# Banded attention, then four experts: loads in another order, x part T4 at the head of its queue, and low halves held back a round

## The chip, the core and the metric

One core of a Trainium2 chip runs the whole program in one launch. The metric is the device time of that launch in microseconds (us); lower is better. The core has five instruction streams that run side by side and wait for each other by semaphores: PE (TensorE, matmuls; its weight loads are listed as PEld), DVE (VectorE), ACT (ScalarE), POOL (GpSimd) and SP, which here only issues transfers. Every stream executes its own instructions strictly in the order in which the program wrote them.

## The reference

```python
# attention: 4 batches, 8 heads, 576 positions, 64 wide
scores = q @ k.T / 8                     # per batch and head
mask_plain = (rel >= 0) & (rel < 32)                       # heads 0..3
mask_dil   = (rel >= 0) & (rel < 128) & (rel % 4 == 0)     # heads 4..7
attn = softmax(where(mask, scores, -1e9))
x = (attn @ v) laid out as [2304, 512]
# mixture of experts: 4 experts, each 512 -> 1024 -> 512
p = domain_probs / domain_probs.sum(-1)
out = sum over e of p[:, e] * (relu(x @ w1[e]) @ w2[e])
```

All of it is float32 with float32 results.

## The kernel before

**Attention** is cut into 24 steps of two groups each (192 queries of a pair of heads). A step needs a load of q (`q_s`) and k (`k_s`, L270), both on SP, and two loads of v (`v_s`, L277). It runs through stages: `s_qk` (scores `sc`, PE, L292), `s_max` (DVE, L306), `s_sub` (POOL, L320), `s_exp` (ACT), `s_sum` (DVE), `s_norm` (POOL, L342), `s_tr` (PE, `pt`), `s_av` (PE, `po`, L373), and ACT copies the result into x. In each *round* (the loop over `n` in the main part) one step is in each stage. q and k have `QKB` = 3 buffers, v has `VB` = 4.

**The experts** are 16 units (four of each expert's four slices of 256 hidden columns), and the 2304 tokens are three blocks m of 768. A *visit* is a unit on a block. Float32 products are made of three products of split numbers: a *high half* (ACT, `HI = copy`, names `xh`, `g1h`, `g2h`, `w2h`, L129) and a *low half*, the rest (POOL or DVE subtract, names `xl`, `g1l`, `g2l`, `w2l`, L126); `split` writes both. The first matmul layer uses a Winograd scheme of seven products (`m1x`, `m1y`, L411) per visit: A12, A11, S2, S1, S3, S4, A22, each with a part of x (B21, B11, T2, T1, T3, B22, T4). The parts T are sums of quarters of x (`x_sums`, DVE, L223), the weights S are sums of quarters of w1 (`w1_sums`, POOL, L160 to L166, in place in the loaded tile `r`). The second layer (`mm2`, result `m`, L514) is scaled into `acc` by DVE (L522). Units 0 and 1 go over block 0 first, with eight plain products each, then units 2 to 15 over block 0 while attention goes on, then all units over blocks 1 and 2.

Weights come in tiles `r`: w1 (L107) with two buffers, w2 (L115) with one. `fetch_w1(u + 2)` is written behind `w1_late(u)`, and `fetch_w2(u + 1)` behind `w2_late(u)`, so SP waits there until POOL has read the buffer (`g2l` or `w2l`); SP's loads written behind them wait as well.

**What sets the order.** Attention's loads stand in the list `loads`; at the head of each round they are issued from its front as long as the buffers allow (`ready`). The splitting of weights and of x goes through `queue`, a list of generators: `step()` takes one step of the first one, and after each piece of expert work (a *tick*) one or two steps are taken; `need(...)` takes steps until a named item is done. From `START` = round 7 to `OPEN` = round 15 (the gate) attention is denser and the experts run two pieces a round; from round 15 on, 11 pieces (`PACE`). `held`, `holding` and `flush()` let `split` write the high half now and the low half later. `dummies` are matmuls without use that keep PE busy early on.

Of the kernel before, what the change touches and what calls it, by code (L numbers as in the profile page):

```python
# [24 lines left out]
VB = 4  # L25
# [24 lines left out]
def kernel(  # L50
# [483 lines left out]
    def experts(begin):  # L534

        for half in range(2):
            for n in ("X12", "B22") if half else ("B11", "B21"):
                for i in range(2):
                    need(x_part, i, n)
            for u in range(2):  # L540
                need(w1_split, u)
                yield from plain((u, 0), half)
                if half:
                    prepare(w1_split, u + 2)
                    prepare(w1_sums, u + 2)
                    if u == 0:
                        prepare(w1_late, 2)
                        fetch_w1(3)
                    else:
                        for j in range(2):  # L550
                            prepare(x_part, j, "T4")
                need(w2_late, u)
                yield from mm2((u, 0), u == 0, False, half, range(2))
                if half:
                    prepare(w2_late, u + 2)
            if half == 0:
                yield from pause("open")
        need(w1_split, visits[0][0])
        yield from mm1_a(visits[0])
        for i, (u, m) in enumerate(visits):  # L560
            blocks = [b for v, b in visits if v == u]
            mine = [v for v in visits if v[1] == m]
            ends = m and (u, m) == mine[0], (u, m) == mine[-1]
            if m == blocks[0]:
                need(w1_late, u)
            yield from mm1_b((u, m))
            if m == blocks[-1] and u < LAST:
                prepare(w1_late, u + 1)
            if (u, m) == (NU - 1, 0):
                for n in ("T3", "T4"):  # L570
                    for j in (4, 5):
                        prepare(x_part, j, n)
            if m == blocks[-1] and u + 2 <= LAST:
                prepare(w1_split, u + 2)
                prepare(w1_sums, u + 2)
            if i + 1 < len(visits):

                need(w1_split, visits[i + 1][0])
                need_x(visits[i + 1][1], ("B11", "B21"))
                opening = mm1_a(visits[i + 1])  # L580
                yield next(opening)
            if m == blocks[0]:
                need(w2_late, u)
            yield from mm2((u, m), *ends, 1)
            if i + 1 < len(visits):
                begin()
                yield from opening
                if visits[i + 1] == (NU - 1, 0):

                    assert "m1" in gate  # L590
                    need(x_sums, 5)
                    for n in ("T2", "T1"):
                        for j in (4, 5):
                            prepare(x_part, j, n)
            yield from mm2((u, m), *ends, 0)
            if m == blocks[-1] and u + 2 <= LAST:
                prepare(w2_late, u + 2)
# [6 lines left out]
    def step(of=None):  # L604
        of = queue if of is None else of
        while of:
            if next(of[0][1], 0) != 0:
                return
            of.pop(0)

    def prepare(what, *args, soon=False, of=None):
        of = queue if of is None else of
        of.insert(0 if soon else len(of), ((what, args), what(*args)))
# [13 lines left out]
    with tc.manual_schedule():  # L627
# [139 lines left out]
        shares = []  # L767
        ready = {"w2": lambda u: u < 1 or (u - 1, 1) in w2_op}
        ready["qk"] = lambda m: m < qk_done + QKB
        ready["v"] = lambda m: m < av_done + VB  # L770

        def load(what, m):
            if what == "qk":
# [8 lines left out]
                (fetch_w1 if what == "w1" else fetch_w2)(m)  # L782

        loads = [
# [5 lines left out]
        ]  # L790
        for m in range(needed[1] + 1, len(steps)):
            loads += [("qk", m), ("v", m)]

        dummies(18)
        ffn = experts(begin)
        for n in range(at(len(steps) - 1) + 5):
            while loads and ready.get(loads[0][0], lambda m: True)(loads[0][1]):
                load(*loads.pop(0))
            if START < n < OPEN:
                flush()  # L800
                holding.add(n)
                step()
                holding.clear()
            for k, order in enumerate(stages):
                for stage, after in order:
                    m = step_at.get(n - after, -1)
                    if m >= 0 and k == (m > needed[1]):
                        stage(m, steps[m])
                        av_done += stage == order[(1, 2)[k]][0]
            if n in step_at:  # L810
                qk_done += 1
            for i, names in when.get(n, ()):
                for name in names:
                    of = first_x if i < 2 else later
                    if name is None or name == "T2":
                        prepare(x_sums, i, of=of)
                    if name is not None:
                        prepare(x_part, i, name.upper(), of=of)
            place = 0 if n <= START or n >= OPEN else len(queue)
            queue[place:place] = first_x  # L820
            first_x.clear()
            if n == 5:
                prepare(w1_split, 0)
            if n == START:
                prepare(w2_late, 0)
                prepare(w1_split, 1)
                weigh(shares[0])
            if n == START + 2:
                prepare(w2_late, 1)
            if n == OPEN:  # L830
                gate.add("open")
            if n < START:
                dummies(FILL)
                step()
                if n > 4:
                    step()
                    step()
                continue
            if "open" not in gate:
                for _ in range(2):  # L840
                    if next(ffn) == "idle":
                        dummies(3)
                    step()
                continue
            for _ in range(PACE if n in step_at else 4):
                next(ffn)
                step()
                if len(queue) > 8:
                    step()
                elif later and len(queue) < 5:  # L850
                    step(later)
# [61 lines left out]
```

## Time and profile before

| | |
|---|---|
| median of 3 runs | 887.48 us (886.26 to 889.19) |
| the profiled execution: its own time | 888.0 us |
| its span, first to last instruction | 886.2 us |
| mean granted TensorE clock | 0.973 |
| PE busy | 833.6 us (94% of the span) |
| DVE / ACT / POOL busy | 479.9 / 315.2 / 390.2 us |
| the chain that ended last | PE 82%, DMA 5% (all of `k_s<-kT`), POOL 4%, DVE 3% |

[...] The 1.8 us between the span and the execution's own time lie outside the instructions.

### The profile page before, as it was taken

The page shows a single profiled execution, that of the slowest core. Times are in us where ns is not written, and L with a number is a line of the kernel's source. Part 1 is how long each engine was busy: PE and PEld are TensorE (multiplying, and loading weights), DVE is VectorE, ACT ScalarE, POOL GpSimd, SP SyncE. Part 2 cuts the span into 40 slices and gives each one's busy share as a digit, 9 for nine tenths or more (in the row PEclk, how much of TensorE's full clock was granted, in tenths as well). Part 3 has the DMA queues.
Part 4 walks back from the last instruction along what each step waited for, and adds up shares of the span by engine and source line. Part 5 has one row for each costly group of instructions (what it writes and reads, how often), then busy time and mean ns, then how long its engine had stood idle before and what let it go on. Part 6 is the DMA issues. An engine that isn't in the chain of part 4 may idle for free.

```text
span 886.2 us, 15444 instructions
## 1 busy us (share of the span) xinstructions
PE 833.6 (94%) x6202; PEld 735.9 (83%) x6202; DVE 479.9 (54%) x1035; ACT 315.2 (36%) x753; POOL 390.2 (44%) x473
## 2 busy tenths in 40 slices
PE   6989699888879999699999999999999999999998
PEld 4778588777767898589999898998989999898997
DVE  3566365744437654865554555455454555555454
ACT  2542434533334444343324223332422333242221
POOL 2463776965536756573234224323423432332310
PEclk9799899999989999799999999999999999999999
DMA  9772222222242221141010101001010100100003
GB/s 260 186 198 59 95 67 86 86 86 85 85 122 86 86 67 51 45 130 37 24 48 24 48 25 48 25 24 47 24 48 25 48 24 24 47 25 25 1 15 128
DMA packets 46610, 59.15 MB, mean 67 GB/s; under 512 B 2873, under 2 KB 36025, under 8 KB 46539
## 3 DMA queue, kind: packets, MB, share of 16 engines
q1 hardware_dynamic: 46123, 57.75, 21.7%
q8 instruction: 48, 0.79, 0.4%
q10 hardware_dynamic: 416, 0.43, 0.1%
q14 instruction: 23, 0.19, 0.1%
HBM read 53.45 MB, written 4.72 MB: 66 GB/s over the span
## 4 chain that ended last, share of the span: by engine, by line
PE 82%; DMA 5%; POOL 4%; DVE 3%; ACT 2%; SPq 1%; issue 1%; POOLq 0%; DVEq 0%
PE m L514 40%; PE m1x L411 22%; PE m1y L411 16%; DMA k_s<-kT 5%; PE po L373 2%; POOL g2l L126 1%; PE sc L292 1%; DVE xr L223 1%; POOL w2l L126 1%; PE pt L353 1%; ACT hh L429 1%; SPq L277 1%; DVE acc L522 1%; POOL sm L320 1%; DVE xl_B L126 1%
## 5 line engine op out<-in xcount | busy, mean ns | idle before, releaser
L522 DVE SCALAR_TENSOR_TENSOR acc<-m,pn,acc 128x512 f32<-128x512 f32 x270 | 202.0, 749 | 142.6 <-PE m L514 142.5
L514 PE MATMUL m<-w2h,hh 128*128 128x512 f32 x576 | 230.1, 399 | 5.9 <-DVE acc L522 4.2
L514 PE MATMUL m<-w2l,hh 128*128 128x512 f32 x576 | 227.2, 394 | 0.0
L126 POOL TENSOR_TENSOR g2l<-r,g2h 128x256 fp32r<-128x256 f32 x120 | 86.6, 753 | 222.2 <-PE m L514 212.5
L514 PE MATMUL m<-w2h,hl 128*128 128x512 f32 x576 | 179.2, 392 | 0.0
L429 ACT ACTIVATE hh<-s 128x384 fp32r<-128x384 f32 x92 | 48.3, 525 | 256.7 <-DVE s L452 197.4
L514 PEld LDWEIGHTS m<-w2h,hh 128*128 128x128 f32 x576 | 109.8, 191 | 29.8 <-DVE acc L522 6.9
L514 PEld LDWEIGHTS m<-w2h,hl 128*128 128x128 f32 x576 | 108.9, 189 | 24.1
L514 PEld LDWEIGHTS m<-w2l,hh 128*128 128x128 f32 x576 | 109.8, 191 | 19.8
L126 POOL TENSOR_TENSOR w2l<-r,w2h 128x512 fp32r<-128x512 f32 x62 | 79.5, 1302 | 87.3 <-ACT w2h L129 87.3
L126 POOL TENSOR_TENSOR g1l<-r,g1h 128x256 fp32r<-128x256 f32 x93 | 70.8, 789 | 92.6 <-ACT g1h L129 92.5
L471 DVE TENSOR_TENSOR s<-m1x,s 128x384 f32<-128x384 f32 x46 | 25.6, 557 | 106.3 <-PE m1x L411 106.3
L462 ACT ACTIVATE u<-m1x 128x384 f32<-128x384 f32 x46 | 22.6, 492 | 156.0 <-PE m1x L411 156.0
L435 DVE SCALAR_TENSOR_TENSOR hl<-s,hh 128x384 fp32r<-128x384 f32 x92 | 52.6, 571 | 27.9 <-ACT hh L429 27.7
L411 PE MATMUL m1x<-xh_T,g2h 128*128 128x384 f32 x152 | 52.0, 342 | 0.7 <-DVE s L452 0.7
L411 PE MATMUL m1x<-xl_T,g2h 128*128 128x384 f32 x152 | 51.5, 339 | 0.0
L411 PE MATMUL m1x<-xh_T,g2l 128*128 128x384 f32 x152 | 51.4, 338 | 0.0
L411 PE MATMUL m1x<-xh_T,g1h 128*128 128x384 f32 x96 | 33.9, 353 | 11.2 <-DVE s L471 7.8
L306 DVE CUSTOM_DVE_ANT_0 sm<-sc,mask 128x64 f32<-128x64 f32 x144 | 22.7, 220 | 36.7 <-PE sc L292 32.7
L411 PE MATMUL m1y<-xl_B,g2h 128*128 128x384 f32 x124 | 41.6, 336 | 0.0
L411 PE MATMUL m1y<-xh_B,g2h 128*128 128x384 f32 x124 | 41.6, 336 | 0.0
L411 PE MATMUL m1y<-xh_B,g2l 128*128 128x384 f32 x124 | 41.4, 334 | 0.0
(122 smaller groups left out, 1515.2 us busy)
## 6 DMA issues: line engine op xcount, KB each, us to landing
r<-w SPq DMA_DIRECT2D x64, 512.0 KB, 3.5
v_s<-vw SPq DMA_DIRECT2D x48, 192.0 KB, 4.7
k_s<-kT SPq DMA_DIRECT2D x23, 224.0 KB, 4.6
q_s<-qT SPq DMA_DIRECT2D x24, 192.0 KB, 4.3
out<-acc SPq DMA_DIRECT2D x18, 256.0 KB, 2.0
k_s<-kT ACTq DMA_DIRECT2D x1, 224.0 KB, 3.6
mask<-masks ACTq DMA_DIRECT2D x1, 192.0 KB, 4.1
pt__427<-probs SPq DMA_DIRECT2D x1, 36.0 KB
```

Of the source, the lines that this page charges most:

```text
L126: lo_eng.tensor_tensor(out=lo, in0=src, in1=hi.bitcast(F32), op=ALU.subtract)
L223: nc.vector.tensor_tensor(out=quarter(i, d), in0=quarter(i, a), in1=quarter(i, b), op=ALU.subtract)
L277: nc.sync.dma_start(out=t[KB * k:KB * (k + 1)], in_=vw[b, p][:, :, gi * GB:(gi + 1) * GB, :])
L306: nc.vector.tensor_tensor_reduce(out=sm[:, i * len(gs) + k, :], in0=banks[k][:, i * KB:(i + 1) * KB], in1=mask[:, which[blk if p < NP // 2 ...
L373: nc.tensor.matmul(po[k][64 * j:64 * j + 64, o:o + QB], v_s[rows, j, 2 * i + half, :], ts_[rows, c:c + QB], start=True, stop=True,)
L411: nc.tensor.matmul(bank, w[:, k], x[:, k], start=(first and k == 0 and i == 0), stop=(last and k == 1 and i == 2), skip_group_check=True,)
L429: nc.scalar.activation(out=hi, in_=src, func=AF.Relu)
L435: nc.vector.scalar_tensor_tensor(out=lo, in0=src, scalar=0.0, in1=hi.bitcast(F32), op0=ALU.max, op1=ALU.subtract)
L462: nc.scalar.activation(out=u2, in_=x, func=AF.Copy)
L471: nc.vector.tensor_tensor(out=s5, in0=x, in1=s5, op=ALU.add)
L514: nc.tensor.matmul(po, h, w, start=(n == 0 and x == 0), stop=(n == 3))
L522: nc.vector.scalar_tensor_tensor(out=acc, in0=po, scalar=pn[:, tt, e:e + 1], in1=acc, op0=ALU.mult, op1=ALU.add,)
```

## The change

The list of loads is put in another order up to step 9 (two lines of it are shown). From step 10 on an entry that has no place yet no longer stops the list: entries behind it are looked at as well; v of a step waits until the scores of the step before it have been written. The first w1 unit is split from round 6 on instead of 5. Part T4 of x for block 0 goes to the head of `queue` (`soon=True`) instead of its end. Before, only the first `step()` of a gated round held its low halves back until the next `need`, `flush` or unheld split; now all splits of rounds 8 to 14 do, and a gated round takes two steps in all instead of three.

```diff
-                        for j in range(2):
-                            prepare(x_part, j, "T4")
+                        for j in (1, 0):
+                            prepare(x_part, j, "T4", soon=True)
...
-        ready["v"] = lambda m: m < av_done + VB
+        ready["v"] = lambda m: m < av_done + VB and (m <= needed[1] or m <= qk_done)
...
-            ("qk", 0), ("masks", 0), ("qk", 1), ("qk", 2), ("v", 0), ("v", 1),
-            ("qk", 3), ("w1", 0), ("v", 2), ("qk", 4), ("v", 3), ("v", 4),
...
+            ("qk", 0), ("masks", 0), ("qk", 1), ("qk", 2), ("v", 0), ("qk", 3), ("v", 1),
+            ("qk", 4), ("v", 2), ("v", 3), ("w1", 0), ("v", 4), ("qk", 5), ("w2", 0),
...
+        def load_ready():
+            at = 0
+            while at < len(loads):
+                what, m = loads[at]
+                if ready.get(what, lambda m: True)(m):
+                    load(*loads.pop(at))
+                elif what == "w2" or m > needed[1]:
+                    at += 1
+                else:
+                    break
...
-            while loads and ready.get(loads[0][0], lambda m: True)(loads[0][1]):
-                load(*loads.pop(0))
+            load_ready()
             if START < n < OPEN:
                 flush()
                 holding.add(n)
                 step()
+            else:
+                flush()
                 holding.clear()
...
-            if n == 5:
+            if n == 6:
                 prepare(w1_split, 0)
...
                     if next(ffn) == "idle":
                         dummies(3)
-                    step()
+                step()
                 continue
```

PE's own instructions stand in the same order before and after. On SP the start of the program changes so (one piece of the difference; `v_s` is two loads for a step, so x4 is two steps):

```order
-L277 DMA v_s<-vw 64x2x384 x4
+L277 DMA v_s<-vw 64x2x384 x2
 L269 DMA q_s<-qT 128x2x192
 L270 DMA k_s<-kT 128x2x224
-L107 DMA r_203<-w 128x4x256
 L277 DMA v_s<-vw 64x2x384 x2
 L269 DMA q_s<-qT 128x2x192
 L270 DMA k_s<-kT 128x2x224
 L277 DMA v_s<-vw 64x2x384 x4
+L107 DMA r_267<-w 128x4x256
+L277 DMA v_s<-vw 64x2x384 x2
```

The second `k_s` of this piece belongs to step 4; before, two more loads of v and the first w1 stood ahead of it.

On SP in the rounds behind the gate, before (`r2` is a w2 tile, `r1` a w1 tile; the two `k_s` belong to steps 15 and 16, the `r2` and `r1` between them to units 7 and 8):

```order
L269 DMA q_s_2239<-qT 128x384
L270 DMA k_s_2240<-kT 128x2x224
L115 DMA r2_2344<-w2 128x2x512
L107 DMA r1_2402<-w1 128x4x256
L277 DMA v_s_2474<-vw 64x2x384 x2
L269 DMA q_s_2477<-qT 128x2x192
L270 DMA k_s_2478<-kT 128x2x224
```

And after (steps 16 and 17; the weights are those of units 6 and 7, then 7 and 8):

```order
L269 DMA q_s_2029<-qT 128x2x192
L270 DMA k_s_2030<-kT 128x2x224
L115 DMA r2_2139<-w2 128x2x512
L107 DMA r1_2187<-w1 128x4x256
L277 DMA v_s_2238<-vw 64x2x384 x2
L269 DMA q_s_2241<-qT 128x384
L270 DMA k_s_2242<-kT 128x2x224
L115 DMA r2_2384<-w2 128x2x512
L107 DMA r1_2436<-w1 128x4x256
```

q and k of step 16 now stand ahead of the weights of unit 6, two pairs of weight loads earlier. By rounds: k of steps 15 to 23 was issued in the round that uses it, and is now issued two rounds ahead.

On POOL around the first visit with sums of weights (unit 2), before (`r_1029` is w1 of unit 2, `r_1373` of unit 3, `xl_T_0_1009` is T4 of x):

```order
L166 TENSOR_TENSOR r_1029<-r_1029 128x2x128
L126 TENSOR_TENSOR g2l<-r_1029,g2h 128x2x128 x2
L320 TENSOR_TENSOR sm<-sm,nm 128x384
L126 TENSOR_TENSOR g2l<-r_1029,g2h 128x2x128 x2
L126 TENSOR_TENSOR w2l<-r_1031,w2h 128x512 x2
L126 TENSOR_TENSOR g1l<-r_1373,g1h 128x256 x3
L160 TENSOR_TENSOR r_1373<-r_1373 128x2x128
L162 TENSOR_TENSOR r_1373<-r_1373 128x2x128
L164 TENSOR_TENSOR r_1373<-r_1373 128x2x128
L166 TENSOR_TENSOR r_1373<-r_1373 128x2x128
L126 TENSOR_TENSOR xl_T_0_1009<-xr,xh_T_0_1008 128x2x192
```

And after (`r_1024` is w1 of unit 2, `xl_T_0_1019` is T4; the two `xl_T` in front are T1 and T3, which stood ahead of the gate before):

```order
L126 TENSOR_TENSOR xl_T_0_1370<-xr,xh_T_0_1369 128x2x192
L126 TENSOR_TENSOR xl_T_0_1382<-xr,xh_T_0_1381 128x2x192
L126 TENSOR_TENSOR g1l<-r_1024,g1h 128x256 x3
L126 TENSOR_TENSOR xl_T_0_1019<-xr,xh_T_0_1018 128x2x192
L160 TENSOR_TENSOR r_1024<-r_1024 128x2x128
L162 TENSOR_TENSOR r_1024<-r_1024 128x2x128
L320 TENSOR_TENSOR sm<-sm,nm 128x384
L164 TENSOR_TENSOR r_1024<-r_1024 128x2x128
L166 TENSOR_TENSOR r_1024<-r_1024 128x2x128
L126 TENSOR_TENSOR g2l<-r_1024,g2h 128x2x128 x4
L126 TENSOR_TENSOR w2l<-r_1026,w2h 128x512 x2
```

T4 moved from behind the sums of unit 3 to ahead of those of unit 2, and two of those sums now stand behind the subtraction of an attention step (L320). In the later units of block 0 the low halves of the S weights stand 8 pieces of expert work ahead of their use before, and 5 after.

## Rows read from the trace of the kernel before

**Rows 1.** Windows: length, busy us per engine (instructions), PE clock, DMA share, GB/s.

```profile
core 0: us, PE busy (x) PEld busy (x) DVE busy (x) ACT busy (x) POOL busy (x), PEclk, DMA share, GB/s
...
103.90:172.50 68.60, 65.80 (x586) 56.65 (x584) 43.57 (x114) 29.97 (x75) 50.13 (x61) 1.00 0.28 88
172.50:262.00 89.50, 73.76 (x775) 63.89 (x775) 37.62 (x119) 31.49 (x81) 49.43 (x61) 0.90 0.34 97
...
378.00:886.20 508.20, 504.16 (x2521) 455.62 (x2519) 269.21 (x425) 161.24 (x368) 166.87 (x204) 1.00 0.12 40
```

**Rows 2.** Waits of PE: line waited for, us in total, times, longest.

```profile
PE sc L292 <- DMA k_s<-kT: 20.7, 8, 6.2
```

**Rows 3.** Timeline of PE: start, length, instruction, [idle before, what ended it].

```profile
192.56 0.84 PE L292 MATMUL sc<-k_s,q_s 64*32 64x64 f32 x48 [2.40 <-DMA k_s<-kT]
...
255.82 0.95 PE L292 MATMUL sc<-k_s,q_s 64*32 64x64 f32 x48 [6.15 <-DMA k_s<-kT]
```

**Rows 4.** Windows again, short stretches; columns as in rows 1.

```profile
12.00:20.00 8.00, 3.59 (x147) 2.80 (x150) 2.13 (x15) 1.72 (x5) 2.35 (x3) 0.92 1.08 244
20.00:32.00 12.00, 12.00 (x241) 9.03 (x226) 5.52 (x23) 5.58 (x16) 3.49 (x4) 0.50 0.98 241
192.50:196.40 3.90, 3.84 (x58) 3.70 (x59) 0.96 (x12) 0.49 (x1) 1.15 (x2) 0.56 0.01 2
...
255.80:259.80 4.00, 3.98 (x55) 3.21 (x56) 1.08 (x13) 0.00 (x0) 0.00 (x0) 0.50 1.02 264
100.50:103.90 3.40, 3.39 (x11) 3.39 (x12) 0.56 (x1) 1.01 (x2) 1.80 (x2) 0.50 0.00 0
```

**Rows 5.** Timeline of SP's queue: start and length of issuing a transfer.

```profile
203.44 0.37 SPq L115 DMA_DIRECT2D r<-w  x1
206.23 0.37 SPq L107 DMA_DIRECT2D r<-w  x1
...
208.52 0.43 SPq L270 DMA_DIRECT2D k_s<-kT  x1
```

**Rows 6.** Timeline of POOL in the same stretch.

```profile
200.86 2.55 POOL L126 TENSOR_TENSOR w2l<-r,w2h 128x512 fp32r<-128x512 f32 x2 [7.14 <-ACT w2h L129]
203.37 2.84 POOL L126 TENSOR_TENSOR g2l<-r,g2h 128x256 fp32r<-128x256 f32 x4
```

**Rows 7.** Timeline of PE: the first S2 product, and A22 with T4.

```profile
88.25 0.45 PE L411 MATMUL m1x<-xh_T,g2h 128*128 128x384 f32 x1 [0.72 <-DVE s L452]
...
95.30 0.44 PE L411 MATMUL m1x<-xh_T,g1h 128*128 128x384 f32 x1 [2.34 <-ACT xh_T L129]
...
100.51 0.69 PE L411 MATMUL m1x<-xl_T,g1h 128*128 128x384 f32 x1 [4.59 <-POOL xl_T L126]
```

**Rows 8.** Timeline of POOL in that stretch.

```profile
78.35 0.74 POOL L166 TENSOR_TENSOR r<-r 128x256 f32<-128x256 f32 x1
...
87.23 0.83 POOL L320 TENSOR_TENSOR sm<-sm,nm 128x384 f32<-128x384 f32 x1
...
99.47 0.99 POOL L126 TENSOR_TENSOR xl_T<-xr,xh_T 128x384 fp32r<-128x384 f32 x1
```

**Rows 9.** Timeline of PE at the start: the scores of steps 3 and 4.

```profile
13.35 0.71 PE L292 MATMUL sc<-k_s,q_s 64*32 64x64 f32 x48 [1.19 <-DMA k_s<-kT]
...
19.46 0.96 PE L292 MATMUL sc<-k_s,q_s 64*32 64x64 f32 x48 [3.23 <-DMA k_s<-kT]
```

**Rows 10.** Timelines of DVE and PE between gate rounds 11 and 12.

```profile
52.65 1.39 DVE L223 TENSOR_TENSOR xr<-xr 128x384 f32<-128x384 f32 x1
...
54.62 0.52 PE L353 MATMUL pt<-ident,sm 128*128 128x128 f32 x3 [1.52 <-DVE nm L306]
```

**Rows 11.** Timelines of DVE and PE near the end of block 0.

```profile
362.38 7.28 DVE L223 TENSOR_TENSOR xr<-xr 128x384 f32<-128x384 f32 x8
...
372.15 0.69 PE L411 MATMUL m1x<-xh_T,g1h 128*128 128x384 f32 x1 [7.77 <-DVE s L471]
```

**Rows 12.** Waits of SP's queue for PE's scores, as in rows 2.

```profile
SPq L269 <- PE sc L292: 6.8, 2, 6.6
```

5 rows, old and new, of the table loads are left out of this document.

## The prediction

> **What bounds the kernel now.** I read the windows first, because they say where PE loses time. From 378.00 to the end PE is busy 504.16 of 508.20 us at clock 1.00 [rows 1]: 4 us are all that could ever be won there, and the change touches nothing in it. From 103.90 to 172.50 PE is busy 65.80 of 68.60 us at full clock; from 172.50 to 262.00, with the same mixture of attention and experts, 73.76 of 89.50 us at a mean clock of 0.90 [rows 1]. So the second stretch loses 15.7 us in idle time and, with 0.10 of the clock missing, about 7.4 us (73.76 × 0.10) in slow matmuls. The list of PE's waits then says for what: scores wait 20.7 us in 8 pieces for `k_s` [rows 2]. The timeline shows two of them, 2.40 and 6.15 us long [rows 3], and the windows behind these two show a clock of 0.56 and 0.50 [rows 4]: each wait is paid twice, as idle time and as half speed for about 4 us.
>
> Why is k late? At 203.44 and 206.23 SP issues a w2 and a w1 tile, and only at 208.52 the k that PE needs next [rows 5]. These two issues end the waits for POOL: `w2l` started at 200.86 and took 2.55 us, `g2l` started at 203.37 and took 2.84 us [rows 6], so SP stands until 203.41 and 206.21. k is not late for want of bandwidth but because it stands behind two loads whose buffers POOL frees.
>
> Elsewhere: PE waits 2.34 and 4.59 us for the two halves of T4, with clock 0.50 for 3.4 us behind it [rows 4, 7]; at the start it waits 1.19 and 3.23 us for k of steps 3 and 4 [rows 9], and the clock is 0.50 from 20 to 32 us [rows 4]; between gate rounds there is a wait of 1.52 us [rows 10]; near the end of block 0 one of 7.77 us [rows 11]. PE's own instructions keep their order, so the change can move the time only through these waits, the clock behind them, and new waits.
>
> **Part by part.** *(a) k two rounds ahead.* In the round shown POOL stands idle for 7.14 us ahead of `w2l` [rows 6], so a round is longer than that, and two rounds far longer than the longest of these waits, 6.2 us [rows 2]: k should be there. It removes 20.7 − 1.19 − 3.23 = 16.3 us of idle time. Behind the two waits shown, the slow stretches cost 3.9 × 0.44 = 1.7 and 4.0 × 0.50 = 2.0 us; the window's mean clock makes it 7.4 us over all. Upper bound: 16.3 + 7.4 = 23.7. Worked from the other side: at full clock the stretch holds 73.76 − 7.4 = 66.4 us of PE work; with PE's share of the clean stretch, 65.80 / 68.60 = 0.959, it takes 69.2 us, a gain of 20.3. A lower bound of 17 supposes that each of the six waits leaves half a microsecond or so of a next wait. What is next: POOL, which is busy 49.43 of 89.50 us now, would have the same work in 69 us, 71% [rows 1]; in the clean stretch it has 50.13 in 68.60 us (73%) and PE does not suffer, so this cover exists. I take **21.0**, nearer to the clean stretch than to the upper bound.
>
> *(b) T4 at the head of the queue.* It removes 2.34 + 4.59 us of waiting and 3.4 × 0.50 = 1.7 us of slow clock: 8.6. It is not free: the sums and `g2l` of unit 2 now stand behind it on POOL, and two of the sums behind the subtraction of an attention step. That subtraction starts at 87.23 and takes 0.83 us, so ends at 88.06; two sums of 0.74 [rows 8] and one `g2l` (2.84 / 4 = 0.71 [rows 6]) make 90.25, whereas the first S2 product starts at 88.25 now [rows 7]. The first high half needs the sums too, so a new wait of about 2.0 us stands there, 3.7 if the clock falls behind it as it did behind T4. A further 0.9 or so I allow for the next unit's first weights, which come behind four `g2l` and two `w2l`; T4's own 0.99 us per piece [rows 8] does not vanish from POOL, it is only done sooner. 8.6 − 2.0 − 0.9 = 5.7 at best, 4.0 with the clock; the net is **5.3**, range 3.5 to 8.6.
>
> *(c) The start.* k of step 4 now has one step of v (384 KB by the tile shapes) and the first w1 (512 KB) less ahead of it, 917,504 bytes; at 244 GB/s [rows 4] that is 3.7 us earlier, against a wait of 3.23. k of step 3 has 384 KB less, 1.6 us, against a wait of 1.19. Both waits together are 4.4 us; some of the second returns as a wait for what the DMA queues bring next, since they are full until 32 us (shares 1.08 and 0.98 [rows 4]), so I take 3.7. Then the clock: it is 0.92 before the 3.23 us wait and 0.50 behind it for 12.00 us, all busy [rows 4, 9]. If it never falls, at most 6 us (half of 12.00) come back; but in that stretch the engines ahead of PE and the full DMA queues set a pace too, so I take 2.0. Sum **5.7**, range 1 to 9.7. The first w1 comes later by some 4 us; its split moves from round 5 to 6 and covers that. Without the cover the first expert products would wait that long.
>
> *(d) Held low halves and one step less in a gated round.* DVE's sum of 1.39 us, which makes `nm` late by 1.52 us for the transposes [rows 10], moves behind the work of attention. About 1.0 comes back, 0.4 is lost where a low half held to the next round is late for its product: **+0.6**, range −3 (two waits like this one added) to +1.5. Beyond the gate the low halves of the S weights have 5 pieces of work ahead of their use where they had 8; I cost that at nothing, since POOL is a quarter idle; what it costs if that fails is a rival.
>
> *(e) The burst at the end of block 0* stays: eight quarter sums of DVE, 7.28 us for 8 [rows 11], and PE waits 7.77. They take 0.91 each there, and 1.39 where POOL works beside them [rows 10]. [...] From rows alone: since block 0 ends sooner and POOL has as much to do, one more sum of eight at 1.39 instead of 0.91 costs 0.5; I take **−0.4**, bounds −3.8 and 0.
>
> Sum: 21.0 + 5.3 + 5.7 + 0.6 − 0.4 = 32.2. The profiled execution took 888.0 us, half a microsecond above the median of 887.48, so 888.0 − 32.2 = 855.8, and I forecast **856**, 3.6% less. Anything within 0.3% (2.7 us) of the time before cannot be told from no change.
>
> **The rivals.** *R1: the clock stays low at the start all the same.* There the work is sparse: PE is busy 3.59 of 8.00 us from 12 to 20 [rows 4]. Then (c) gives only the 3.7 us of idle time, and the sum is 30.2: 858. Speaking for it, nothing makes PE denser there; against it, that same sparse stretch had 0.92. [...]
>
> *R2: the shorter lead.* If 5 pieces instead of 8 are too few, PE waits for `g2l` or `w2l` once in each of the 12 visits of units 4 to 15 to block 0; at the size of the nearest such wait, 1.52 [rows 10], that is 18 us: 856 + 18 = 874. For it: the queue takes no more steps than before and has less time for them. Against it: POOL is a quarter idle.
>
> *R3: k does not come earlier in fact*, because SP, in order, still stands at a weight load while a k waits behind it. Then (a) is nothing: 877. Against it: the order on SP has q and k of step 16 two pairs of weight loads further up.
>
> *R4, slower: weights late instead of k.* An entry whose turn has come now stands on SP ahead of the weights, and q and k wait for their own buffers, which PE's scores free (today SP waits 6.8 us for these in 2 waits [rows 12]). If in each of the 14 visits of units 2 to 15 the weights come so late that PE waits, this outweighs the gain from 32.2 / 14 = 2.3 us a visit on: 888 and above. Against it: in the rounds shown the load that PE lacked was k, never a weight.
>
> **How the numbers follow.** Forecast 0.50, with a range of its own from 849 to 862 (the bounds of (a) and (c) together); R1 0.25 (852 to 865); R2 0.12 (866 to 880); R3 0.07; R4 0.06. The first two and a little of R2 make eight in ten: 848 to 868. Faster by over 0.3%: all but R4 and a little of R2 and R3 together with mishaps, 0.92; within 0.3% 0.03; slower 0.05.
>
> **What would show it.** (a) the waits for `k_s` fall from 20.7 to under 3 us, and what is now the stretch from 172.50 runs at clock 1.00; R3 if they stay. (b) no wait for `xl_T` of T4, and one of about 2 us before the first S2 product. (c) scores of step 4 near 16 us instead of 19.46 and a clock near 1.00 from 20 to 32; 0.50 there is R1. (d) the wait of 1.52 gone. (e) a wait of 7 to 8 us remains near the end of block 0. R2 shows as many waits of PE for `g2l` or `w2l`; R4 as waits of the weight splits for `r` and long waits of SP for scores. The prediction is wrong if waits of another name take the place of those for k, above all between 160 and 250 us.

## The result and the profile after

858.08 us (median of 4 runs, 856.0 to 858.93) against 888.08 for the kernel before (4 runs, 886.26 to 889.19): a ratio of 0.9661, interval 0.9635 to 0.9686, 30.0 us less. The profiled execution has a span of 857.1 us against 886.2, 29.1 less.

PE executes the same instructions in the same order in both kernels, so its instructions serve as milestones. The first fence is the windows view of the kernel before, cut at the scores of steps 5, 10, 12, 16 and 23 and at the product behind the last stall of block 0; the second is the kernel after, cut at the same instructions. Columns as in [rows 1].

```profile
0.00:35.29 35.29, 28.00 (x571) 20.17 (x571) 14.57 (x86) 13.06 (x33) 11.01 (x19) 0.81 0.88 228
35.29:70.85 35.56, 31.09 (x599) 25.33 (x598) 24.58 (x98) 14.68 (x37) 18.64 (x21) 1.00 0.66 188
70.85:109.26 38.41, 30.64 (x229) 26.12 (x229) 18.16 (x49) 14.22 (x35) 24.04 (x28) 0.91 0.21 64
109.26:174.37 65.11, 61.88 (x614) 53.42 (x613) 41.31 (x111) 29.98 (x75) 48.49 (x58) 1.00 0.29 89
174.37:308.51 134.14, 116.16 (x1156) 100.09 (x1156) 70.51 (x194) 51.39 (x132) 79.14 (x96) 0.94 0.31 91
308.51:372.15 63.64, 55.87 (x501) 49.67 (x501) 38.93 (x70) 26.76 (x69) 40.48 (x48) 0.96 0.18 57
372.15:886.20 514.05, 510.01 (x2538) 461.12 (x2538) 271.87 (x430) 165.07 (x376) 168.43 (x205) 0.99 0.12 40
```

```profile
0.00:35.86 35.86, 27.88 (x572) 19.81 (x572) 16.10 (x88) 13.01 (x32) 10.98 (x19) 0.83 0.84 224
35.86:70.51 34.65, 33.06 (x598) 27.65 (x597) 21.41 (x95) 13.76 (x35) 16.42 (x19) 0.93 0.60 182
70.51:102.19 31.68, 28.75 (x229) 24.60 (x228) 17.46 (x49) 13.43 (x32) 22.02 (x25) 1.00 0.26 74
102.19:167.21 65.02, 61.56 (x613) 53.29 (x612) 43.63 (x111) 31.14 (x77) 50.63 (x59) 1.00 0.33 104
167.21:277.95 110.74, 109.29 (x1157) 94.19 (x1156) 75.16 (x194) 52.79 (x133) 80.50 (x95) 1.00 0.34 102
277.95:342.39 64.44, 56.18 (x502) 49.66 (x501) 42.31 (x70) 28.50 (x72) 46.74 (x53) 0.97 0.20 63
342.39:857.10 514.71, 510.76 (x2538) 461.27 (x2538) 273.14 (x430) 165.13 (x376) 168.09 (x205) 0.99 0.12 40
```

Length for length, the stages gain −0.57, +0.91, +6.73, +0.09, +23.40, −0.80 and −0.66 us, in all 29.1. Nearly everything comes from two stages: the one with the waits for k (idle time from 17.98 to 1.45 us, busy time from 116.16 to 109.29 for the same work, as the clock goes from 0.94 to 1.00) and the one with T4. The start gains nothing. (The expectations below have 23.3 for the stage with the waits for k: there it was cut a step earlier.)

That k is early, and not merely in time, shows at one step: SP issued k of step 18 at 208.52 [rows 5] for scores at 212.78 before, and at 165.08 for scores at 198.66 after.

PE's waits after, the groups that matter here (line waited for, us in total, times, longest), and its timeline at the places the prediction named:

```profile
PE m1x L411 <- DVE s L471: 7.7, 1, 7.7
PE po L373 <- issue: 4.7, 2, 4.1
...
PE m1x L411 <- ACT g2h L129: 1.6, 1, 1.6
...
PE m1x L411 <- POOL g2l L126: 1.0, 2, 0.6
```

```profile
12.62 0.73 PE L292 MATMUL sc<-k_s,q_s 64*32 64x64 f32 x48
15.46 0.72 PE L292 MATMUL sc<-k_s,q_s 64*32 64x64 f32 x48
...
21.33 0.55 PE L373 MATMUL po<-pts,v_s 64*64 64x32 f32 x24
26.01 0.86 PE L373 MATMUL po<-pts,v_s 64*64 64x32 f32 x24 [4.13 <-issue]
...
88.78 0.45 PE L411 MATMUL m1x<-xh_T,g2h 128*128 128x384 f32 x1 [1.58 <-ACT g2h L129]
89.65 0.44 PE L411 MATMUL m1x<-xh_T,g2l 128*128 128x384 f32 x1 [0.43 <-POOL g2l L126]
...
95.94 0.44 PE L411 MATMUL m1y<-xh_B,g1l 128*128 128x384 f32 x1 [0.81 <-POOL g1l L126]
...
342.39 0.69 PE L411 MATMUL m1x<-xh_T,g1h 128*128 128x384 f32 x1 [7.65 <-DVE s L471]
```

No wait for `k_s` is left, where [rows 2] had 20.7 us, and none for T4, where [rows 7] had 2.34 and 4.59. The scores of step 4 start at 15.46, where [rows 9] had 19.46. New is a wait that the prediction did not have at all: 4.13 us at 26.01, in the middle of the products of one step, and released by "issue", that is, by nothing that the profile shows. What it does to the clock is seen in the windows:

```profile
12.00:20.00 8.00, 7.43 (x264) 5.70 (x262) 5.07 (x34) 3.71 (x10) 4.15 (x6) 1.00 1.02 245
20.00:32.00 12.00, 7.87 (x125) 6.23 (x122) 3.35 (x9) 5.36 (x16) 2.33 (x3) 0.66 0.98 255
...
172.00:250.00 78.00, 77.82 (x827) 67.26 (x826) 49.94 (x133) 37.49 (x92) 57.05 (x68) 1.00 0.37 108
```

From 12 to 20 us the clock is now 1.00 and PE is busy 7.43 of 8 us, against 3.59 [rows 4]. From 20 to 32 it falls again, to 0.66, behind the new stall (0.50 from 26.01 to 35.86, with PE busy 9.44 of 9.85 us). From 172 to 250 PE is busy 77.82 of 78 us at full clock.

### The profile page after: what moved, and what is told of

Its sections match the earlier page's. It is cut to its first block, busy times and chain, and to the rows that moved or that the text cites. A ratio compares the mean times of both kernels' runs of the same rounds, so it can differ in the third digit from the quotient of the medians.

```text
span 857.1 us, 15475 instructions
## 1 busy us (share of the span) xinstructions
PE 827.5 (97%) x6202; PEld 730.5 (85%) x6202; DVE 489.2 (57%) x1035; ACT 317.7 (37%) x753; POOL 395.4 (46%) x473
## 4 chain that ended last, share of the span: by engine, by line
PE 90%; DVE 5%; POOL 1%; ACT 1%; issue 1%; DVEq 0%; POOLq 0%
PE m L514 44%; PE m1x L411 23%; PE m1y L411 17%; PE po L373 2%; PE sc L292 1%; PE wt L743 1%; PE pt L353 1%; DVE xr L223 1%; DVE acc L522 1%; DVE xl_B L126 1%; DVE hl L435 1%; ACT hh L429 0%; DVE sm L306 0%; POOL g1l L126 0%; POOL xl_T L126 0%
## 5 line engine op out<-in xcount | busy, mean ns | idle before, releaser
L514 PE MATMUL m<-w2h,hh 128*128 128x512 f32 x576 | 227.7, 395 | 4.9 <-DVE acc L522 4.5
L435 DVE SCALAR_TENSOR_TENSOR hl<-s,hh 128x384 fp32r<-128x384 f32 x92 | 58.4, 635 | 27.6 <-ACT hh L429 27.5
L129 ACT ACTIVATE g2h<-r 128x256 fp32r<-128x256 f32 x120 | 41.4, 405 | 0.3 <-POOL r L164 0.3
```

Of the source, the lines that this page charges most:

```text
L129: nc.scalar.activation(out=hi, in_=src, func=AF.Copy)
L435: nc.vector.scalar_tensor_tensor(out=lo, in0=src, scalar=0.0, in1=hi.bitcast(F32), op0=ALU.max, op1=ALU.subtract)
L514: nc.tensor.matmul(po, h, w, start=(n == 0 and x == 0), stop=(n == 3))
```

## The experiments

Each kernel was timed in five rounds against the kernel before on the same chip; ratios are to it, and the kernel after stands at 0.9661. A thousandth is 0.9 us. The intervals are some 0.2 to 0.35 per cent to either side, so terms of a few us are read from the milestones as well.

Two questions were open: where each term comes from, for which the parts of the change are undone or made alone; and what PE waits for at 26.01. Theory A: PE has no instructions there; they arrive late, over the DMA engines that the loads keep full (shares 1.02 and 0.98 from 12 to 32 us). Rival B: the second half of v of that step lands late.

### Only the start undone

```diff
-            ("qk", 0), ("masks", 0), ("qk", 1), ("qk", 2), ("v", 0), ("qk", 3), ("v", 1),
-            ("qk", 4), ("v", 2), ("v", 3), ("w1", 0), ("v", 4), ("qk", 5), ("w2", 0),
+            ("qk", 0), ("masks", 0), ("qk", 1), ("qk", 2), ("v", 0), ("v", 1),
+            ("qk", 3), ("w1", 0), ("v", 2), ("qk", 4), ("v", 3), ("v", 4),
+            ("qk", 5), ("w2", 0), ("probs", 0), ("qk", 6), ("w1", 1), ("v", 5),
...
-            if n == 6:
+            if n == 5:
                 prepare(w1_split, 0)
```

> The changed kernel with the order of the first loads (and the round of the first w1 split) as before; the rest of the change stays. In the changed kernel PE stands for 4.13 us at 26.01, in the middle of the products of one step, ended by nothing that the profile shows; step 5's scores start at 35.86 there and at 35.29 before. Theory A: that stall eats what the new order wins (instructions of PE arrive late over the same full DMA engines), so the order of the first loads is worth nothing: 858 less 0.6 for the scores and less up to 2.0 for a clock that is at its upper level again after 33 us, so 855.5 to 858. Rival, my prediction's term: the order is worth 5.7 us, so the time rises to 863 to 864.

857.45 us (856.32 to 858.52), ratio 0.9651, interval 0.9619 to 0.9682. The waits for k are back (2.01 and 1.08 us) and the 4.13 us are gone. The order of the first loads is worth nothing that can be measured in this kernel: theory A's number, not the 5.7 us of my term.

### Only the list that passes entries over, on the kernel before

```diff
-        ready["v"] = lambda m: m < av_done + VB
+        ready["v"] = lambda m: m < av_done + VB and (m <= needed[1] or m <= qk_done)
...
-            while loads and ready.get(loads[0][0], lambda m: True)(loads[0][1]):
-                load(*loads.pop(0))
+            load_ready()
```

> The kernel before with the passing-over of loads alone (and the new condition on v), nothing else of the change. Theory: the gain from k of steps 15 to 23 is the list's alone, 21 by the prediction and 23.3 by the two traces between the scores of steps 16 and 23: 888.1 - 23 = 865, between 863 and 867; waits of PE for k_s fall to the 4.4 us at the start. Rival: without T4 ahead and the low halves held, POOL is later in the queue and part of the gain goes: 870 to 874.

863.97 us (862.09 to 868.19), ratio 0.9737, interval 0.9702 to 0.9773. The waits for `k_s` are 2.3 us, both at the start, and the clock from 172 to 262 is 1.00. The list alone brings some 23 us, as expected; the waits for T4 (2.34 and 4.19) are still there.

### The list undone, the rest kept

The same lines the other way round.

> The changed kernel without the passing-over of loads and without the new condition on v; the rest of the change stays. Theory: the list alone brings the 23 us between the scores of steps 16 and 23, so 880 to 883, with waits of PE for k_s near 16 us again and clock below 0.95 in the stretch. Rival: part of the 23 us comes from the other parts (POOL less in arrears, so the weight loads ahead of k are issued sooner), 870 to 877.

885.22 us (882.62 to 889.44, 12 runs), ratio 0.9981, interval 0.9960 to 1.0002: the rest of the change without the list is hardly worth anything. That is above both expectations. The list of waits of this kernel:

```profile
PE sc L292 <- DMA k_s<-kT: 21.2, 7, 4.9
```

All seven stand behind 148 us (before, six did, with 16.3 us in all). So the other parts make k come even later where the list doesn't bring it ahead; taken away, the list costs 28 us (0.9981 less 0.9661), added by itself it gives 23 (1 less 0.9737). The 28 us all lie where k is waited for: between the scores of steps 12 and 23 this kernel takes 203.77 us and the kernel after 175.76. Why the two prices differ by 5 us was not taken apart further; k's waits alone are 4.9 us longer here than the 16.3 of the kernel before.

### T4 back at the end of the queue

```diff
-                        for j in (1, 0):
-                            prepare(x_part, j, "T4", soon=True)
+                        for j in range(2):
+                            prepare(x_part, j, "T4")
```

> The changed kernel with T4 of block 0 at the end of its queue again, as before. My prediction's term is 5.3 us, the two traces give 6.7 between the scores of steps 10 and 12: 863 to 865, with waits of PE for xh_T and xl_T of T4 of 2 and 4 to 5 us again and the wait of 1.58 before the first S2 product gone. Rival: with k early and the low halves held, POOL has time for T4 where it stood, and nothing is lost: 858.

865.25 us (861.81 to 867.41), ratio 0.9740, interval 0.9704 to 0.9775: T4's place is worth 7.0 us; from the scores of step 10 to those of step 12 it takes 39.92 us, 8.2 more than the kernel after. Its timeline of PE:

```profile
89.60 0.45 PE L411 MATMUL m1x<-xh_T,g2h 128*128 128x384 f32 x1 [1.58 <-ACT g2h L129]
...
97.09 0.44 PE L411 MATMUL m1x<-xh_T,g1h 128*128 128x384 f32 x1 [2.34 <-ACT xh_T L129]
102.12 0.69 PE L411 MATMUL m1x<-xl_T,g1h 128*128 128x384 f32 x1 [4.40 <-POOL xl_T L126]
```

The two waits for T4 are back. But the wait of 1.58 us before the first S2 product, which I had put down to T4 standing ahead on POOL, stays. It has another cause (below). It stays with any one part of the change undone (start, list, T4 or holding) and is 0.72 us, as before, with the list alone, so no single part is its only source.

### Holding of low halves undone

```diff
                 flush()
                 holding.add(n)
                 step()
-            else:
-                flush()
                 holding.clear()
...
-                step()
+                    step()
```

> The changed kernel with the holding of low halves and the steps of a gated round as before. By the prediction the part is worth 0.6 us; between the scores of steps 5 and 10 the trace of after has 2.9 us less idle time of PE, and 2.0 us more busy time at a clock of 0.93 that comes from the stall at 26 us. Theory: undone, the waits for hh near 40 us (1.30) and for nm near 54 us (1.52) are back, 859 to 861. Rival (the shorter lead costs in the later units of block 0, since there the low halves are 5 pieces ahead instead of 8): undone, the time falls below 857.

860.04 us (857.68 to 861.61), ratio 0.9687, interval 0.9657 to 0.9717. One stage tells more than the sum; its scores of step 5 start at 35.77 behind the same stall of 4.13 us, those of step 10 at 73.15:

```profile
35.77:73.15 37.38, 34.45 (x599) 28.75 (x598) 22.56 (x95) 14.53 (x36) 17.76 (x20) 0.89 0.57 168
```

That is 37.38 us where the kernel after takes 34.65, with 2.93 us idle instead of 1.59: the wait for `nm` (1.51) is back, while the one for `hh`, against my expectation, is not. The other 1.39 us are the clock's, 0.89 against 0.93. The part is worth 2.3 us by the ratios, whose intervals overlap, and 2.7 by the milestones of one pair of traces, 1.3 of it idle time. A pair with the clock at 1.00 in both is the kernel with only the start undone, which holds the halves, and the one with the list alone, which does not; their first loads stand in the same order, and T4 comes behind this stage (first the one that holds):

```profile
36.38:69.48 33.10, 31.05 (x599) 25.49 (x598) 21.53 (x96) 13.77 (x35) 16.43 (x19) 1.00 0.68 190
31.49:67.00 35.51, 31.07 (x598) 25.33 (x598) 24.54 (x98) 14.66 (x37) 18.64 (x21) 1.00 0.62 180
```

Here the holding saves 2.4 us, all of it idle time (the kernel before, without it too, takes 35.56). The rival, that the shorter lead costs time later, would have made the kernel without the holding the faster one.

### Fewer instructions, then more, for the same columns at the start

The matmuls without use (`wt`) have 256 columns. Here are half as many of 512, and twice as many of 128 (the edit shown is the first; its last line also gives two idle places later on 512 such columns instead of 768):

```diff
-FILL = 6
+FILL = 3
...
-                nc.tensor.matmul(wt[:, :256], warm[:, :128], warm, start=True, stop=True)
+                nc.tensor.matmul(
+                    wt.rearrange("p (a b) -> p a b", a=2), warm[:, :128],
+                    warm.unsqueeze(1).to_broadcast([128, 2, 256]), start=True, stop=True,
+                )
...
-        dummies(18)
+        dummies(9)
...
-                        dummies(3)
+                        dummies(1)
```

> The changed kernel with half as many matmuls without use at the start, each with 512 columns in place of 256: PE has the same columns to do with some 50 instructions fewer by 22 us. Theory A (PE waits for its own instructions): PE stops again at the instruction that is number 961 of its matmuls and weight loads (705 and 961 are where it stopped, 256 apart), which is now a later matmul of the program, about 2 us later; the stall of 4.13 shrinks to 1 to 3 us, step 5's scores start 1 to 3 us sooner, 855 to 857. Rival B (the second half of v of that step lands late): PE stops at the same matmul (the second 24 of one step's products po) for 4 us again, 858.

> The changed kernel with twice as many matmuls without use, each with 128 columns in place of 256: the same columns, some 100 instructions more by 22 us. Theory A (PE waits for its own instructions): it stops at instructions 705 and 961 of its matmuls and weight loads as in the other kernels, but these stand earlier in the program; the stalls are longer or more, and step 5's scores start 2 to 6 us later than at 35.86: 860 to 864. Rival B (a late load of v): the same columns give the same stall at the same matmul, 858.

Half as many: 853.73 us (852.5 to 855.82), ratio 0.9611, interval 0.9579 to 0.9644. Twice as many: 863.65 us (863.11 to 865.15), ratio 0.9733, interval 0.9704 to 0.9761. The first gained more than expected; in the second only one of the two expected stalls came. Their timelines of PE, first the kernel with half as many, then the other:

```profile
22.95 0.55 PE L353 MATMUL pt<-ident,sm 128*128 128x128 f32 x3
24.63 0.82 PE L743 MATMUL wt<-ident 128*128 128x512 bf16 x3 [1.14 <-issue]
```

```profile
19.46 0.41 PE L292 MATMUL sc<-k_s,q_s 64*32 64x64 f32 x18
21.83 0.45 PE L292 MATMUL sc<-k_s,q_s 64*32 64x64 f32 x30 [1.96 <-issue]
```

The stall has moved: to a `wt` matmul that reads no v at all, and into the middle of a step's scores. A late v is out. What stays the same is the count. The windows from the program's start to the stall, of the kernel after (its 0.57 us wait at 17.09, then its 4.13), with half as many, and with twice as many (its 1.96):

```profile
0.00:16.53 16.53, 13.65 (x347) 8.74 (x348) 7.00 (x57) 4.73 (x9) 6.39 (x14) 1.00 0.89 250
0.00:21.93 21.93, 18.44 (x474) 12.35 (x474) 10.04 (x75) 8.03 (x18) 9.31 (x18) 1.00 0.93 247
```

```profile
0.00:23.55 23.55, 19.43 (x474) 11.66 (x474) 10.58 (x76) 8.62 (x21) 10.00 (x18) 0.86 0.99 273
```

```profile
0.00:19.90 19.90, 18.13 (x348) 12.32 (x348) 7.10 (x57) 4.84 (x9) 6.42 (x14) 1.00 0.81 232
```

Read the two counts of PE and PEld: 474 + 474 = 948 in two kernels whose programs differ, and 347 + 348 = 695, or 696, at the other place: 253 apart. (The expectations say 961 and 705, 256 apart; they count PE's few semaphore instructions too.) The traces of all the kernels here have 22 such waits of PE over 0.15 us, and every one stands at 449, 705, 961, 1985 or 2241 by that count, whole multiples of 256 apart.

### The first weights later

```diff
-            ("qk", 4), ("v", 2), ("v", 3), ("w1", 0), ("v", 4), ("qk", 5), ("w2", 0),
-            ("probs", 0), ("qk", 6), ("w1", 1), ("v", 5), ("qk", 7), ("v", 6), ("w2", 1),
+            ("qk", 4), ("v", 2), ("v", 3), ("v", 4), ("qk", 5), ("probs", 0),
+            ("qk", 6), ("w1", 0), ("v", 5), ("qk", 7), ("v", 6), ("w2", 0), ("w1", 1), ("w2", 1),
```

> The changed kernel with the first weights later in the list: w1 of unit 0 behind q and k of step 6, w2 of unit 0 and w1 of unit 1 behind v of step 6. Theory A: less stands in the DMA queues when PE asks for its next instructions near 17 us, so the stall of 4.13 us falls below 1.5 us and the clock does not fall at 26 us; with the 2.7 and 3 us of half speed behind the stall back that is 849 to 854. Rival C: w1 is late instead, PE waits 3 us or more for g1h at the first expert products near 31 us: 857 to 860.

857.88 us (855.72 to 859.08), ratio 0.9652, interval 0.9620 to 0.9685: the same as the kernel after. Its timeline and window:

```profile
17.27 0.77 PE L373 MATMUL po<-pts,v_s 64*64 64x32 f32 x37 [1.23 <-issue]
...
25.48 0.87 PE L373 MATMUL po<-pts,v_s 64*64 64x32 f32 x24 [1.44 <-issue]
```

```profile
0.00:24.10 24.10, 19.91 (x474) 13.45 (x474) 10.74 (x76) 8.04 (x18) 10.00 (x18) 0.89 0.94 257
```

Both stalls stand at the same counts. The second is shorter by 2.7 us, but PE also came to it later, since the first was longer; the instructions arrive at about the same time (PE goes on at 25.48, against 26.01). My expectation that they would come sooner was wrong, and so was rival C, whose time this is: PE does not wait for `g1h`. The reading that remains, from the DMA share alone: other loads take the place of the weights in queues that are full either way (share 0.94 here, 0.93 in the kernel after).

### Both: fewer instructions and later weights; fewer instructions and the old order

> The kernels thin and late_w together: fewer instructions for PE, and the first weights later in the list. Theory: with the weights later, PE's instructions come no sooner (late_w's block came at 24.1 us against 24.7), so nothing more than thin's 853.7: 852.5 to 855. Rival: the two add up, 850 to 852.

854.58 us (853.31 to 855.69), ratio 0.9628, interval 0.9599 to 0.9657: nothing on top of fewer instructions.

> The kernel thin (half as many matmuls without use, of 512 columns) with the order of the first loads and the round of the first w1 split as before. Against thin's 853.7 this is what the order of loads is worth when PE's instructions arrive nearly in time. Theory: the order then gives what the prediction said, 3.7 us of waits for k and 2 us of clock, so 857 to 860 here, with waits for k_s of 2 to 4 us at the start. Rival: the start is bound by what the DMA brings in all, whatever the order, so 852 to 855.

854.75 us (852.65 to 859.27), ratio 0.9634, interval 0.9601 to 0.9666, against 0.9611 in the new order: at most some 2 us, and the intervals overlap. That is the rival's time, but the intervals do not tell the two expectations apart; the wait for k that the theory wanted is there (4.4 us in the profiled execution, the slowest of its runs).

### No matmuls without use in the first rounds

```diff
-FILL = 6
+FILL = 0
```

> The changed kernel without the six matmuls without use in each round before the gate rounds (the 18 at the very start stay): some 60 instructions fewer for PE by 22 us, and 3 us fewer columns at full clock. Theory A (instructions late): PE comes to instruction 961 only after its block has arrived, no stall of that kind of more than 0.5 us at 961; the time depends on the clock, which has less to keep it up: 852 to 858. Rival: the matmuls without use are what keeps the clock up, and without them the first 33 us run at half speed: 860 or more.

859.71 us (857.25 to 860.71), ratio 0.9681, interval 0.9651 to 0.9711. There is no stall at 948 any more, as theory A said. But the clock is 0.50 from 12 to 32 us, as the rival said, and the time is no better. A stall of 1.81 us released by "issue" stands at 63.31 instead, at 2241 by the count that has 961 above, five times 256 further on.

### Two steps of the queue in the round that opens the gate, with fewer instructions

```diff
-                if len(queue) > 8:
+                if len(queue) > 8 or n == OPEN:
```

> The kernel thin with two steps of the queue instead of one behind each piece of expert work in the round in which the gate opens. The first high halves of the S weights of unit 2 then stand on ACT ahead of the hh that they stand behind now. Theory: the waits of 1.58 and 0.43 us at the first S2 product come from that place on ACT, not from the sums on POOL (these end 1.9 us before the first split starts); they fall below 0.5 together and the time to 851.5 to 853. Rival: the sums on POOL are late, and a wait of 1 us or more stays: 853 to 855.

853.75 us (853.14 to 856.2), ratio 0.9625, interval 0.9595 to 0.9654. In the kernel after, ACT and POOL at that place are these (one fence each):

```profile
87.89 0.52 ACT L429 ACTIVATE hh<-s 128x384 fp32r<-128x384 f32 x1 [1.66 <-DVE s L452]
88.32 1.32 ACT L129 ACTIVATE g2h<-r 128x256 fp32r<-128x256 f32 x4
```

```profile
85.74 0.73 POOL L166 TENSOR_TENSOR r<-r 128x256 f32<-128x256 f32 x1
```

The last sum ends at 86.47, but the split of the S weights starts only at 88.32: on ACT it stands behind `hh`, which waits for DVE. In the experiment two of the four splits stand ahead of that `hh`, and its timeline of PE has 0.72 us there, as before:

```profile
83.64 0.45 PE L411 MATMUL m1x<-xh_T,g2h 128*128 128x384 f32 x1 [0.72 <-DVE s L452]
```

From the scores of step 10 to those of step 12 it takes 30.57 us (66.25 to 96.82) where the kernel with fewer instructions alone takes 32.14 (63.51 to 95.65). The 1.6 us don't show in the median, which is the rival's time and not the theory's; in the profiled execution the start was slower by 2.7 us, and no run shows whether that holds for the others.

## Why the prediction was right, and where it was not

**The total**: 856 forecast, 858.1 measured, on the forecast case; 32.2 us expected from the span, 29.1 found there. That it came so near is partly luck, since misses cancel: the first two stages gave 0.3 us where (c) and (d) have 6.3, the stages of (b) and (a) gave 3.9 more than forecast, and what lies behind them 1.1 less. And the forecast's upper end of 862 is too low for its own terms: the lower bounds 17 and 1 of (a) and (c) make 864.5.

**(a) k ahead, 21.0 forecast, 23.4 found** between the scores of steps 16 and 23: right, and close to the upper bound of 23.7. The stretch came out denser than the clean one from which I took 0.959: 109.29 busy of 110.74. The two experiments with and without the list show that it is the list that does it.

**(b) T4, 5.3 forecast, 6.7 found** in the trace and 7.0 by undoing it: inside its range. The new wait was forecast at 2.0 and is 1.58 + 0.43; the one at the next unit's first weights at 0.9 and is 0.81. But the mechanism of the first was wrong. I counted POOL's sums and forgot ACT's order: `g2h` must follow the sums and is written behind `hh`. The wait stands there without T4 in front too. So 2.0 was the right size by luck, and is no price of T4 alone.

**(c) The start, 5.7 forecast with a range from 1 to 9.7, nothing found**: this is the step that failed. Its first half held: k of steps 3 and 4 is there in time, the scores of step 4 start at 15.46, and the clock is 1.00 until 20 us, so R1 had the low clock (0.66 from 20 to 32) but not its cause: it falls behind the new stall, while R1 had sparse work from 12 to 20 us in mind. Its number, 858, is met by luck: the 3.7 us of idle time that it kept were not won either. What failed is "some of the second returns as a wait for what the DMA queues bring next …, so I take 3.7", with 2.0 for the clock on top. The whole gain is lost again to the stall of 4.13 us and the clock of 0.50 behind it, which reaches into the next stage (33.06 us busy for work that took 31.09). PE runs out of instructions: shown by the stall's fixed place in the count of instructions, whatever stands there, and by the packets that end it (below). The reading that it is the full DMA queues that hold them back is supported by rows (below) but was not separated by a run; the one that tried, with later weights, left the queues as full. That part of the cause stays open.

**(d) Held low halves, +0.6 forecast, 1.3 to 2.4 us of idle time found**: right mechanism, and a term that was too small. With the new order of the first loads 1.3 us come back, near the 1.0 that I counted for `nm`; with the old order, at full clock, it is 2.4. The 0.4 that I subtracted did not show. The 1.4 us that the clock gave when the part was undone are of one pair of traces, and no run separates them from the start's.

**(e) The burst, −0.4 forecast, −0.8 found**, of which 0.61 is a wait for `g2l` just ahead of it. The wait of 7.65 us stayed. DVE's eight sums took longer, as feared, 8.08 us against 7.28 [rows 11]:

```profile
331.82 8.08 DVE L223 TENSOR_TENSOR xr<-xr 128x384 f32<-128x384 f32 x8
```

But the prices were misread: 0.91 is a mean of two kinds of sums. The windows of the kernel before, DVE's sums alone, show six and then two:

```profile
362.38:368.48 6.10, 5.88 (x6) 0.87 0.00 0
368.48:369.66 1.18, 1.12 (x2) 0.50 0.00 0
```

POOL ends its work there at 368.06. So a sum takes 0.98 us beside POOL and 0.56 without it; the 1.39 of [rows 10] is not the price of all. After, POOL is busy 7.77 of the 8.08 us, and all eight take 1.01 in the mean: two more sums beside POOL are the 0.8 us. That all eight take 1.39, the bound of −3.8, no run shows. PE's wait behind the burst did not grow, since PE came to it later, by the wait for `g2l`.

**R2 and R4** did not happen in any size that counts. Waits for `g2l` are 1.0 us in all, and undoing the hold made it slower. SP does wait more for PE's scores, 14.5 us in 3 waits against 6.8 [rows 12], as R4 said, and the weight splits wait for `r` for 3.0 us in all (ACT 0.6, POOL 2.4) against 1.8; of PE's waits only the 0.61 us for `g2l` follows one of these. R3 is excluded: with the list, no wait for k behind the start.

## What to carry to other kernels

A wait that disappears is only won if whatever PE reaches sooner is there sooner as well (the scores of step 4 started 4.0 us earlier, those of step 5 0.57 later); ask what is next in line at every wait, the instruction stream included. When a wait's releaser is "issue", count the instructions up to it: a stall that stays at one count while the program around it changes is no data wait (here at 948 with a stall of 4.13 us, and at 948 with half as many matmuls without use and 1.14 us). And loads that are in arrears behind another engine's buffer release cost twice here, in idle time (17.98 us against 1.45 in the stage with the waits for k) and in the clock behind it (0.94 against 1.00); letting the ready ones pass was worth more than all else here.

## What was not expected of the hardware

PE's instructions come over the DMA as well. The page of the kernel after has a queue of kind "instruction" (packets, MB, share of the 16 engines), and the DMA view from 23 to 25 us shows one packet of it (23.60 to 24.66), ahead of PE's restart at 26.01, beside a share of data above 1:

```profile
q8 instruction: 49, 0.80, 0.4%
```

```profile
q1 hardware_dynamic: 654, 0.69, 103.5%
q8 instruction: 1, 0.02, 3.3%
...
v_s<-vw SPq DMA_DIRECT2D x1, 192.0 KB, 8.0
```

49 packets for PE's 12,404 matmuls and weight loads are 253 each, near the distance between the two stalls (the kernel before has 48 for as many, 258 each), and 0.80 MB / 49 is 16 KB. In the kernel after, the two stalls end 1.41 and 1.35 us behind the end of such a packet (15.68 and 17.09, 24.66 and 26.01). Each of the 22 stalls ends 1.2 to 1.7 us behind the end of such a packet, with half as many matmuls without use (the packet ends at 23.27, PE restarts at 24.63) as with twice as many (20.31 and 21.83): it is the packet that PE waits for. Why it is late is less sure. From one border, a count at which the stalls stand, to the next PE takes 5.4 us here (16.53 to 21.93), while the load of v in the fence takes 8.0 us to land; the packet that ended the long stall began 6.5 us after PE had passed the border before (17.09 to 23.60), and from 100 us on, where the stages have a DMA share of 0.34 and less, none begins more than 2.4 us behind a border. That early and this dense, with 253 matmuls and weight loads in 5.4 us, PE was faster than its own code arrived; from 70.51 us on, with some 209 matmuls and weight loads in 10 us (2,313 in the 110.74 us of the stage with the waits for k), the kernel after has no such wait.

The start also varies by several us between executions. The kernel with the list alone has the loads of before up to there, yet the scores of step 5 started at 31.49 us in its profile and at 35.29 in that of before. A term of 2 us at the start cannot be read from one pair of traces. The fastest kernel run here is the one with half as many matmuls without use, 853.73 us: against the experiments on the same chip (856.32 to 858.52 with the start undone, 855.72 to 859.08 with later weights) its runs, 852.5 to 855.82, lie lower by some 4 us.
